# A Mamba-2 scan feeding a gated feed-forward layer: steps by pairs of sequences in the first block, scans spread over the block's end, one more row set by TensorE, the first weight piece in halves, the later pieces converted in the loop

## The chip, the cores and the metric

One core of one Trainium2 chip. The metric is the device time of one execution in microseconds (us), the median of several executions. The profile counts from the core's first to its last instruction, about 1.8 us less than the time of the same execution. All positions below are us from the start of that span. TensorE is called PE in the profile, VectorE DVE, ScalarE ACT, GpSimd POOL, the queue that issues transfers SP.

## The reference, cut to what matters

```python
# attention part: x (4, 8, 768, 32), a (4, 8, 768), B and C (4, 8, 768, 16), float32
for c in range(nc):                              # chunks along the sequence
    L = exp(cum[i] - cum[j]) * causal            # products of a between j and i
    y_intra = ((C @ B.T) * L) @ x
    y_inter = (C @ state) * exp(cum)
    state   = decay_full * state + sum(B x decay_from_j)
# bridge: (batch, head, seq, dim) -> x of shape (3072, 256)
h = x @ w_in                                     # w_in (256, 2048), stored as float64
g = h * cos(h)
return g @ w_out                                 # w_out (2048, 256), stored as float64
```

The weights arrive as float64. They are turned into float32 on the chip with integer operations, piece by piece, before TensorE can use them.

## The kernel before: the parts that the change and the argument touch

The 768 positions are six blocks of 128. A block holds the four sequences, 512 tokens. It has 16 steps: in step n a first product `h = x w_in` for 128 (block 0) columns of w_in or for two times 128 columns and two of four sequences (later blocks), then k, w, sin and the gate on ACT and DVE, and two steps later (LAG = 2) the second product with w_out. The argument follows each engine's instructions in program order; on what that rests is said in point 3 of the section on the prediction.

A weight piece is 2 of 16 column blocks; in0, in1 are the first pieces of w_in, out0, out1 those of w_out. A hole is a time in which TensorE waits. A fill is a matmul on ones whose result nobody uses; it only keeps TensorE busy. yT is ACT's copy of the scan's output, which the first product reads. `grade` puts Abs and `last` on ACT and a clip on POOL, `join` two operations on DVE and an add on POOL:

```python
def grade(which, i, later=False):
    ...
    ACT.activation(mag, high.bitcast(FP32), AF.Abs)
    G.tensor_scalar(out=mag, in0=mag, scalar1=MOST, scalar2=LEAST, op0=ALU.min, op1=ALU.max)
    ...
    def rest():
        ACT.activation(last, low, AF.Copy, scale=2.0 ** -29)
def join(which, i):
    ...
    V.tensor_scalar(out=bits, ..., op0=ALU.logical_shift_left, op1=ALU.bitwise_and)
    V.scalar_tensor_tensor(out=bits, in0=high, scalar=0xC0000000, in1=bits, ...)
    G.tensor_tensor(out=dst.bitcast(U32), in0=bits, in1=last, op=ALU.add)
order = [(w, i) for i in range(NPC) for w in ("in", "out")]     # in0 out0 in1 out1 ...
```

The end of the prologue and the loop:

```python
    join(*order[0])                 # in0
    grade(*order[2])                # in1
    intra(0, 3)
    finish(0, 2, "o", 1)
    grade(*order[1])                # out0
    finish(0, 3, "o", 2)            # all four sequences of block 0 are done here
    fill(...)
    join(*order[2])
    join(*order[1])
    ...
    for n in range(NC * NF + LAG):
        ...
        first(n)
        if n == 1:
            ...                     # sum_up of chunk 0
        if n + 3 < len(order):
            rest = grade(*order[n + 3], later=True)
        if n + 2 < len(order):
            join(*order[n + 2])     # out1 in step 1, in2 in step 2, out2 in step 3 ...
        gate(n)
        ...
        if n >= LAG:
            second(n - LAG)
        if c + 1 < NC:              # scan of the next chunk: a sequence each 3 steps, from step 2
            b, j = divmod(f - 3, 3)
            ...
```

## Time and profile before

| what | value |
|---|---|
| time, median of 3 at first (4 with the change's runs) | 397.08 (397.11) us |
| the execution that was traced | 399.58 us, span 397.8, mean granted clock 0.988 |
| TensorE busy | 388.4 us, 98% |
| first product of step 0 in the trace | 24.79 |
| first second product in the trace | 31.52 |

The prediction below shows the page, the chain of waits, the start and the clock. A busy TensorE column counts latency that overlaps with the next matmul (a product of L457 has a mean of 384 ns on the page, but eight of them take 1.73 in the chain), so lengths are taken from the chain, where pieces stand end to end.

### The profile page before, as it was taken

The page shows a single profiled execution, that of the slowest core. Times are in us where ns is not written, and L with a number is a line of the kernel's source. Part 1 is how long each engine was busy: PE and PEld are TensorE (multiplying, and loading weights), DVE is VectorE, ACT ScalarE, POOL GpSimd, SP SyncE. Part 2 cuts the span into 40 slices and gives each one's busy share as a digit, 9 for nine tenths or more (in the row PEclk, how much of TensorE's full clock was granted, in tenths as well). Part 3 has the DMA queues.
Part 4 walks back from the last instruction along what each step waited for, and adds up shares of the span by engine and source line. Part 5 has one row for each costly group of instructions (what it writes and reads, how often), then busy time and mean ns, then how long its engine had stood idle before and what let it go on. Part 6 is the DMA issues. An engine that isn't in the chain of part 4 may idle for free.

```text
span 397.8 us, 7670 instructions
## 1 busy us (share of the span) xinstructions
PE 388.4 (98%) x2926; PEld 321.5 (81%) x2926; DVE 266.4 (67%) x411; ACT 177.9 (45%) x341; POOL 248.0 (62%) x369
## 2 busy tenths in 40 slices
PE   8899999999999999999999999999999999999994
PEld 3446666669889889998889988889988888999994
DVE  7659999974877764776763677773676774444443
ACT  3746666534444344443443433444344443444431
POOL 5556657893665854966764775774665673665751
PEclk9889999999999999999999999999999999999998
DMA  9989799977000398100199000081010010010101
GB/s 100 236 219 238 202 261 175 190 124 97 20 2 0 95 198 80 28 2 0 47 231 95 18 11 0 2 231 35 2 28 0 2 26 2 2 26 2 27 3 26
DMA packets 107365, 30.69 MB, mean 77 GB/s; under 512 B 76512, under 2 KB 103232, under 8 KB 107328
## 3 DMA queue, kind: packets, MB, share of 16 engines
q1 hardware_dynamic: 106272, 29.94, 37.6%
q10 hardware_dynamic: 1056, 0.26, 0.4%
q8 instruction: 23, 0.38, 0.4%
q14 instruction: 14, 0.11, 0.1%
HBM read 26.85 MB, written 3.34 MB: 76 GB/s over the span
## 4 chain that ended last, share of the span: by engine, by line
PE 79%; DVE 10%; issue 4%; ACT 3%; SPq 2%; DMA 1%; DVEq 0%; ACTq 0%
PE hp L457 36%; PE o L548 31%; PE g L370 3%; PE y L402 3%; DVE w L463 2%; SPq L118 2%; PE y L393 2%; DVE gT L470 1%; PE o L512 1%; DVE mag L204 1%; DVE lam L338 1%; DMA bc<-in_C_dram 1%; DVE mag L206 1%; PE hp L447 1%; ACT w L468 1%
## 5 line engine op out<-in xcount | busy, mean ns | idle before, releaser
L457 PE MATMUL hp<-yT,w_in 128*128 128x256 f32 x640 | 154.6, 384 | 0.0
L457 PEld LDWEIGHTS hp<-yT,w_in 128*128 128x128 f32 x640 | 115.5, 190 | 19.8 <-issue 6.1
L496 POOL TENSOR_TENSOR gd<-gT 128x256 f32<-128x256 f32 x79 | 70.8, 896 | 96.6 <-DVE gT L470 96.6
L470 DVE TENSOR_TENSOR gT<-hp,w 128x512 f32<-128x512 f32 x96 | 66.3, 690 | 71.3 <-ACT w L468 69.2
L468 ACT ACTIVATE w<-w,quarter 128x512 f32<-128x512 f32 x96 | 69.3, 722 | 89.1 <-DVE w L463 89.1
L461 ACT ACTIVATE k<-hp 128x512 int32<-128x512 f32 x96 | 57.4, 598 | 105.5 <-PE hp L457 98.9
L463 DVE SCALAR_TENSOR_TENSOR w<-hp,k 128x512 f32<-128x512 f32 x96 | 65.6, 683 | 46.4 <-ACT k L461 45.8
L548 PE MATMUL o<-words,gd 128*128 128x128 f32 x480 | 66.7, 275 | 0.0
L548 PEld LDWEIGHTS o<-words,gd 128*128 128x128 f32 x480 | 60.0, 192 | 0.0
L338 DVE TENSOR_TENSOR_SCAN lam<-arow,unit 128x512 f32<-128x512 f32 x40 | 57.5, 1439 | 0.0
L498 POOL TENSOR_TENSOR gd<-gT,gd 128x128 f32<-128x128 f32 x79 | 49.5, 627 | 6.2
L548 PEld LDWEIGHTS o<-w_out,gT 128*128 128x128 f32 x320 | 48.2, 191 | 4.4 <-DVE ps L562 0.3
L548 PE MATMUL o<-w_out,gT 128*128 128x128 f32 x320 | 49.0, 275 | 0.1
L499 POOL TENSOR_TENSOR gd<-gT,gd 128x128 f32<-128x128 f32 x79 | 36.0, 456 | 6.2
L383 DVE TENSOR_TENSOR m<-g,lam 128x512 f32<-128x512 f32 x48 | 30.7, 680 | 3.0 <-POOL mag L186 1.9
L512 PEld LDWEIGHTS o<-w_out,gT 128*128 128x128 f32 x128 | 24.3, 190 | 9.3 <-issue 6.7
L447 PE MATMUL hp<-yT,w_in 128*128 128x512 f32 x64 | 30.9, 608 | 0.7 <-DVE gT L470 0.7
L548 PE MATMUL o<-w_out,gd 128*128 128x128 f32 x160 | 30.9, 275 | 0.0
L548 PE MATMUL o<-words,gT 128*128 128x128 f32 x160 | 30.9, 275 | 0.0
L512 PE MATMUL o<-w_out,gT 128*128 128x256 f32 x128 | 30.2, 379 | 0.0
L548 PEld LDWEIGHTS o<-words,gT 128*128 128x128 f32 x160 | 24.3, 192 | 0.0
L548 PEld LDWEIGHTS o<-w_out,gd 128*128 128x128 f32 x160 | 24.3, 192 | 0.0
(90 smaller groups left out, 345.1 us busy)
## 6 DMA issues: line engine op xcount, KB each, us to landing
arow<-a_cut SPq DMA_DIRECT2D x20, 512.0 KB
words<-in_moe_w_in_dram SPq DMA_DIRECT2D x8, 512.0 KB
words<-in_moe_w_out_dram SPq DMA_DIRECT2D x8, 512.0 KB
out_dram<-sum SPq DMA_DIRECT2D x20, 128.0 KB
xr<-in_x_dram SPq DMA_DIRECT2D x4, 512.0 KB
along<-a_all SPq DMA_DIRECT2D x20, 64.0 KB
xr<-in_x_dram SPq DMA_DIRECT2D x8, 128.0 KB
bc<-in_B_dram SPq DMA_DIRECT2D x4, 256.0 KB
```

What stands on the lines that cost most here:

```text
L338: V.tensor_tensor_scan(out=lam[c, b][:, hs].rearrange("p h i -> p (h i)"), data0=rows_.rearrange("p h i -> p (h i)"), data1=unit.rearrange ...
L447: PE.matmul(hp[n], lhsT=w_in[:, k, f * P:(f + 1) * P], rhs=yT[c][:, k], start=(k == 0), stop=(k == KT - 1))
L457: PE.matmul(to_[:, e], lhsT=w_in[:, k, fs], rhs=y[:, k, u], start=(k == 0), stop=(k == KT - 1), skip_group_check=True)
L461: ACT.activation(k, hp[n], AF.Copy, bias=0.25, scale=INV_2PI)
L463: V.scalar_tensor_tensor(out=w, in0=hp[n], scalar=INV_2PI, in1=k, op0=ALU.mult, op1=ALU.subtract)
L468: ACT.activation(cos, cos, AF.Sin, bias=quarter, scale=TWO_PI)
L470: V.tensor_tensor(out=gT[n], in0=hp.pop(n), in1=cos, op=ALU.mult)
L496: E.tensor_tensor(out=d[:, 0:2], in0=g[:, 1:2].to_broadcast([P, 2, P]), in1=g[:, 3::-3], op=ALU.subtract)
L498: E.tensor_tensor(out=d[:, 2], in0=g[:, 0], in1=d[:, 0], op=ALU.subtract)
L499: E.tensor_tensor(out=d[:, 3], in0=g[:, 2], in1=d[:, 2], op=ALU.subtract)
L512: PE.matmul(o[c][b], lhsT=g[:, b * P:(b + 1) * P], rhs=w_out[:, f], start=(f == 0 and b % 2 == 0), stop=(f == NF - 1), skip_group_check=True)
L548: PE.matmul(at[q], lhsT=a_[q], rhs=w[q], start=(j == 0 and q in starts), stop=(j == NJ - 1), skip_group_check=True)
```

## The change

Its intent: step 0 needs only sequences 0 and 1 if a step takes the tokens of one pair of sequences, as in the later blocks, so the feed-forward part can begin before sequence 3 is ready. The first weight piece in halves makes that early start possible. All rows of `a` for chunk 0 are spread by TensorE instead of one by a broadcast load. Scans of later chunks move towards the end of the block and over it. And the pieces after the first are converted in the loop, each near the step that uses it. The diff, cut to its core:

```diff
-    fill(warm[:, 0:2])
+    spread_a(0, "h")
     ...
-    grade(*order[0]) ... join(*order[0]); grade(*order[2]) ... grade(*order[1]); finish(0, 3, "o", 2)
-    fill(...); join(*order[2]); join(*order[1])
+    grade("in", 0, n=2)                  # two halves
+    ...
+    join("in", 0); finish(0, 2, "o"); intra(0, 3)
     ...
+    piece = {n: ("out", n // 2) if n % 2 else ("in", n // 2 + 1) for n in range(NF)}
+    FROM, EACH = 7, 4
+    EARLY = 4
     for n in range(NC * NF + LAG):
         first(n)                         # block 0: sequences 0, 1 in even steps, 2, 3 in odd ones
-            join(*order[n + 2])
-            gate(n)
+            for m in ((n,) if n < EARLY else ()) + ((n + 1,) if n >= EARLY - 1 else ()):
+                rests.append(grade(*piece[m], later=True))
+            if n >= EARLY and n in piece:
+                join(*piece[n])
+            gate(n)
+            for r in rests: r()
+            if n < EARLY:
+                if n == 0:
+                    first_scan()         # sequence 3's y, its copy on ACT, the sums of chunk 0
+                join(*piece[n])          # in1 in step 0, out0 in step 1, in2, out1
         ...
-            b, j = divmod(f - 3, 3)      # scans
+            c, j = divmod(n + 1 - FROM - EACH * b, NF)   # four steps each, from step 6
```

## The prediction

> **What bounds the kernel now.** I read the page first (busy shares, clock, costliest groups), then the busy times by window, then the timeline of the first 50 us, then the chain of waits. All times are us from the span's start unless marked ns.
>
> The page, engine shares and the rows of the matmuls:
> ```profile
> PE 388.4 (98%) x2926; PEld 321.5 (81%) x2926; DVE 266.4 (67%) x411; ACT 177.9 (45%) x341; POOL 248.0 (62%) x369
> ...
> L457 PE MATMUL hp<-yT,w_in 128*128 128x256 f32 x640 | 154.6, 384 | 0.0
> ...
> L447 PE MATMUL hp<-yT,w_in 128*128 128x512 f32 x64 | 30.9, 608 | 0.7 <-DVE gT L470 0.7
> ...
> L512 PE MATMUL o<-w_out,gT 128*128 128x256 f32 x128 | 30.2, 379 | 0.0
> ```
> TensorE is the bound. The means include latency that overlaps, so a matmul's cost is read from the chain of waits instead, where a stream's pieces stand end to end:
> ```profile
> 104.24 1.56 PE o L548 x14
> 105.80 0.64 PE g L370 x8
> 106.44 1.92 PE hp L457 x8
> 108.37 1.56 PE o L548 x14
> 109.93 0.38 PE y L393 x8
> 110.30 0.57 PE y L402 x16
> 110.88 0.11 PE s_ps L419 x8
> 110.99 1.93 PE hp L457 x8
> ...
> 114.48 0.11 PE tp L351
> 114.58 0.11 PE tp L352
> 114.69 1.73 PE hp L457 x8
> ```
> From block 1 on there is no hole: one piece starts where the other ends. Eight records of 256 columns cost 1.73; a sequence's scan costs TensorE 0.22 + 0.64 + 1.06 and two slower starts of 0.19, together 2.3. A block-0 step is a first product of 1.73 (four records of 512, or eight of 256: the same) and a second of 1.73, so 3.46. Four scans in a block are 9.2. These are matmuls that the change only moves. So time can come only from the start, from holes in block 0, and from the clock.
>
> The start, in the timeline (third column engine, then line):
> ```profile
> 16.93 1.08 PE L402 MATMUL y<-m,xr 128*32 128x128 f32 x16
> 18.02 1.73 PE L370 MATMUL g<-cT,bcT 32*128 32x256 f32 x8
> ...
> 24.79 3.67 PE L447 MATMUL hp<-yT,w_in 128*128 128x512 f32 x8
> ...
> 29.73 1.96 PE L447 MATMUL hp<-yT,w_in 128*128 128x512 f32 x4 [0.69 <-DVE gT L470]
> ...
> 31.52 1.89 PE L512 MATMUL o<-w_out,gT 128*128 128x256 f32 x8
> ```
> The first product of step 0 starts at 24.79, those of step 2 at 29.73, the second product of step 0 at 31.52. From step 2 to block 1's first product (88.4) are 58.7; the work in it is 14 steps of 3.46 and 9.2 of scans, 57.6. So block 0 has only about 1 us of holes after 29.73 and 0.9 before. The same stretch keeps VectorE full too, and here is the clock:
> ```profile
> 16.00:17.00 1.00, 1.00 (x13) 0.38 (x16) 0.00 (x0) 0.89 (x4) 0.86 (x3) 0.70 0.83 279
> 22.00:23.00 1.00, 1.00 (x3) 0.82 (x4) 0.69 (x1) 1.00 (x3) 0.00 (x0) 0.50 1.05 393
> 30.00:35.00 5.00, 5.00 (x17) 2.88 (x16) 4.93 (x11) 4.11 (x7) 2.75 (x3) 1.00 0.99 262
> 50.00:60.00 10.00, 10.00 (x67) 5.89 (x66) 9.53 (x17) 7.06 (x14) 5.26 (x7) 1.00 0.95 261
> ```
> Columns: length, busy PE, PEld, DVE, ACT, POOL, then granted clock, DMA share, GB/s. DVE is 9.53 of 10 in 50 to 60; the clock was 0.50 from about 16.4 to 23.
>
> **What the skill says.** (1) "TensorE: Matmul & The Clock Gate", What's actually happening: the array's clock is halved after an idle window of about 3.4 us and restored after a busy one. The trace agrees: it fell after a hole at 14.1 to 15.3 amid small row- and column-tiled matmuls, and rose at 23.1 after the fills. (2) Same page, Architectural detail: ScalarE and VectorE are strict first-in-first-out, only weight loads are pulled ahead. The trace agrees: step 1's ACT k (29.32) waits behind the weight conversion's "last" (28.77), although its matmuls ended at 28.3. So I can schedule by program order. (3) "SBUF — State Buffer", Who interferes with whom: VectorE and GpSimd exclude each other on a shared port pair; L204 takes 409 to 1485 ns here, 416 median, which fits.
>
> **The change, part by part.**
>
> *Prologue.* A separate row0 (256 KB, whose wait cost VectorE 1.00 at 6.35) goes; sequence 0 is spread by TensorE as the others. I put the first scan some 0.35 earlier (6.6 for 6.95), the four at 1.14 end at 11.15, and m of sequence 0 is done at 12.4, of sequence 1 at 13.7 (before 15.05: TensorE no longer stands at the third turn). The a_in load is moved behind, and with row0 gone sequence 3's B lands 1 to 2 earlier than 15.28. Then ACT sets the pace: turn 2's copies end near 15.0, the first piece in halves (four of about 0.37) 16.5, yT of sequence 1 at 17.3, turn 3's copies 18.2, then intra 3 (0.65), which stands ahead of step 0 in TensorE's queue. VectorE joins the halves at 16.75 to 17.95, GpSimd adds (half of 1.27 each) to 18.75: just hidden. First product of step 0: T = 19.3 with a full clock, 20.3 with half. Gain: 5.5, less 0.65 for sequence 3's y, which now follows step 0: 4.85.
>
> *Steps 0 to 6, the new latency.* Before, pieces in0, in1 and out0 were all joined before step 0 or right at it. Now in1 is joined in step 0, out0 in step 1, in2 in 2, out1 in 3, each after that step's gate. One link each from the trace: first product 1.73 and 0.22 until ACT sees it, k 0.6, w 0.7, sin 0.76, gate 0.7, join 0.42 + 0.69, add 1.27 and 0.15 of hand-overs; Abs and last 0.67 each on ACT. Relative to T:
> - Step 0: k to 2.55, Abs to 3.2, sin to 4.0, last to 4.7, and only then the copy of yT for sequence 3, to 5.0. Step 1 multiplies sequences 2 and 3, so it starts at 5.1. TensorE ended its sums at 3.05: hole 2.0.
> - in1's add ends at 7.3; step 2's product starts 7.4: hole 0.4. It ends at 9.15.
> - Step 1: product to 6.9, gate to 9.9, out0 joined to 11.0, added to 12.4. The second product of step 0 stands next in the queue: hole 3.3, start at 12.5, so 31.8 absolute against 31.52 before. The whole earlier start is used up here.
> - Step 3: product 14.2 to 16.0, two Abs ahead of its sin, gate to 19.6, out1 added 22.1; the second product of step 2 could start at 19.45: hole 2.6.
> - From step 4 the join stands ahead of the gate; out2 (step 5) still comes 0.4 late.
> - Later, VectorE has per four steps 4 x (0.68 + 0.69 + 1.37) + 5.3 of scan = 16.3 against TensorE's 4 x 3.46 + 2.3 = 16.1: balanced; I allow 1.5 for out pieces a little late.
>
> Sum of holes 10.2. Before's holes in the same stretch were 1.9.
>
> *Scans moved.* Sequences 2 and 3 of each later chunk go into the next block's first half, which needs only sequences 0 and 1. TensorE's 2.3 per sequence is then paid there: 0 net. VectorE is relieved at the end of block 0, where the holes were only the 1 us credited above. The last block's tail is the same code.
>
> *Cut rows.* a_cut leaves some 10 later, so transfers pause near 21 to 29; what follows is 9.8 MB, at 235 GB/s 42, done near 70; each piece and chunk-1 row is needed 10 or more after it lands. Hidden.
>
> Sum with a full clock: -4.85 + 10.2 - 1.9 = +3.45.
>
> *Clock.* The prologue stays thin on TensorE and has one fill instead of five, so I expect the half clock again around 16.4: T 1.0 later and the first product 1.7 longer, 2.7, taken at 0.6: +1.6. The holes of 2 and 3.3 may bring it down once more; about +2 at half a chance: +1. That makes +6; since the change keeps step order, buffers and constants tuned, I leave 0.6 for what I don't see in it: **+5.4, 402.5 us.**
>
> **Rivals.** *The earlier start carries through:* if out0 and in1 came ready sooner than I have it (ACT and VectorE back to back take some 0.1 less per instruction than their records), the holes shrink to 4 and the result is 392 to 395. For it: all engines have spare time in 20 to 30 (VectorE 5.47 of 10). Against: it is a chain of dependences, not of busy time. *VectorE is the bound of block 0*, and moving two scans out (10.6 of VectorE's time) frees as much: 390 to 393. For it: VectorE stands in most of the chain from 30 to 84. Against: TensorE had its next piece back to back in 46 to 75, so it can't go faster. *The clock falls twice or more:* each fall halves the rate for some 3.4 to 7; 406 to 409. For it: fewer fills, longer holes. Against: 28.2 to 29.7 was thin too and kept 1.00. *Late weights by DMA:* would add several us, but nothing in before waits for a piece longer than 0.2.
>
> **Range and chances.** From 396 (half of my holes don't appear, clock mostly full) to 408 (all appear and two falls). Faster by 2% needs 389.1, more than the start and all holes of block 0 together would plausibly give: 0.05. Slower by 2% is over 405.0, my sum plus one fall of the clock: 0.29. Within: 0.66.
>
> **What would show it.** Step 0's first product near 19 to 21; a TensorE hole ended by POOL's add into w_out before the first second product (near 32) and another before that of step 2; step 1 released by the ACT copy of yT; block 1's first product near 93, with two scans still to come; blocks 1 to 4 at 61.9 each as before; the clock at 0.5 around 17 to 23. I am wrong if the first second product starts before 29, if the holes are under 4 together, or if a later block's length changes by over 0.5.

## The result, and the profile after

407.38 us (406.68 to 408.06, 4 runs) against 397.11. The ratio is 1.0259, 95% interval 1.0237 to 1.0282: slower. Ratios here are the mean time of one kernel's fast runs over the mean of the other's fast runs of the same rounds, so they are not quite the ratio of the medians quoted beside them.

The page of the changed kernel, the engine shares and the two groups of products, to be compared with the lines of the prediction:

```profile
PE 387.3 (95%) x2986; PEld 332.4 (82%) x2986; DVE 263.2 (65%) x410; ACT 178.2 (44%) x343; POOL 249.3 (61%) x373
...
L462 PE MATMUL hp<-yT,w_in 128*128 128x256 f32 x768 | 187.6, 388 | 2.0 <-ACT yT L411 2.0
...
L519 PE MATMUL o<-w_out,gT 128*128 128x256 f32 x128 | 32.3, 397 | 9.3 <-POOL w_out L217 9.3
```

No engine has much more to do; only the weight loads (PEld) grow, by 10.9 us, and e5 below finds no cost in that. TensorE has 11.3 us of waits that were not there: 2.0 for a copy of yT, 9.3 for POOL's add into w_out. (Gone are 2.0 of before's: 0.7 for gT, 1.3 for transfers in the prologue.) The chain of waits of the changed kernel shows how the first two come about (start, length, what; "issue" is a hand-over):

```profile
18.52 2.09 PE hp L462 x8
20.61 0.02 issue
20.63 0.61 ACT k L466
21.24 0.02 issue
21.26 0.70 DVE w L468
21.96 0.02 issue
21.99 0.72 ACT w L473
22.71 0.55 ACT last L191
23.26 0.26 ACT yT L411
...
26.54 0.61 ACT k L466
...
28.68 0.57 issue
29.26 0.43 DVE mag L207
29.69 0.02 issue
29.71 0.70 DVE mag L209
...
30.55 1.28 POOL w_out L217
```

Step 0 starts at 18.45, over 6 us before the traced kernel's 24.79. But step 1 needs the yT copy, which stands behind Sin and `last` in ACT's order. And the first second product needs out0, whose join stands behind step 1's gate in DVE's order. In the timeline of TensorE, the second products that wait (length of the wait in brackets):

```profile
31.87 3.38 PE L519 MATMUL o<-w_out,gT 128*128 128x256 f32 x8 [2.89 <-POOL w_out L217]
42.67 2.00 PE L519 MATMUL o<-w_out,gT 128*128 128x256 f32 x8 [2.23 <-POOL w_out L217]
50.50 2.00 PE L519 MATMUL o<-w_out,gT 128*128 128x256 f32 x8 [0.66 <-POOL w_out L217]
77.47 2.00 PE L519 MATMUL o<-w_out,gT 128*128 128x256 f32 x8 [2.47 <-POOL w_out L217]
94.20 2.00 PE L519 MATMUL o<-w_out,gT 128*128 128x256 f32 x8 [0.33 <-POOL w_out L217]
```

The first of them starts at 31.87; before it started at 31.52. The early start is gone by the time the second products begin. The one at 31.87 also takes 3.38 instead of 2.00. The windows show why (busy time of PE, PEld, DVE, ACT, POOL, then granted clock, DMA share, GB/s):

```profile
20.00:24.00 4.00, 2.05 (x53) 1.53 (x52) 1.92 (x4) 2.70 (x5) 0.61 (x1) 1.00 0.32 117
24.00:28.00 4.00, 4.00 (x13) 3.16 (x12) 1.38 (x3) 1.26 (x3) 1.99 (x4) 0.57 0.10 27
28.00:32.00 4.00, 1.11 (x6) 0.66 (x4) 2.58 (x6) 2.92 (x6) 1.83 (x3) 0.91 0.92 197
32.00:36.00 4.00, 4.00 (x13) 3.31 (x14) 1.98 (x5) 0.58 (x2) 1.66 (x2) 0.66 0.83 216
```

In this trace the clock is down after each of these two stretches in which TensorE had little to do (2.05 of 4, then 1.11 of 4). The hole of 2.23 ahead of 42.67 was not followed by a fall.

The wait of 2.47 at 77 has its own history, in the timeline of POOL:

```profile
70.71 1.27 POOL L217 TENSOR_TENSOR w_in<-mag,last 128x512 uint32<-128x512 uint32 x1 [0.63 <-DVE mag L209]
71.94 1.40 POOL L494 TENSOR_TENSOR words<-w_out 128x512 f32<-128x512 f32 x1
73.31 1.52 POOL L194 TENSOR_SCALAR mag<-mag 128x512 f32<-128x512 f32 x1
76.15 1.26 POOL L217 TENSOR_TENSOR w_out<-mag,last 128x512 uint32<-128x512 uint32 x1 [1.32 <-DVE mag L209]
```

and of DVE:

```profile
72.19 2.23 DVE L342 TENSOR_TENSOR_SCAN lam<-arow,unit 128x512 f32<-128x512 f32 x1
```

A difference of w_out (L494) and a clip that takes 1.52 instead of 0.61 run against a scan that takes 2.23 instead of 1.2: POOL and DVE hold each other up there, as the Trainium skill, "SBUF — State Buffer", Who interferes with whom, describes for a DVE instruction with two SBUF inputs and a POOL instruction that reads SBUF. The trace agrees: the scan ends 1.08 after the difference (74.42 and 73.34), about what it takes elsewhere, and the clip ends 0.41 after the scan. The join follows late, and with it TensorE; e8 tests how much of that is due to the differences.

### The profile page after: what moved, and what is told of

Its sections match the earlier page's. It is cut to its first block, busy times and chain, and to the rows that moved or that the text cites. A ratio compares the mean times of both kernels' runs of the same rounds, so it can differ in the third digit from the quotient of the medians.

```text
span 406.1 us, 7789 instructions
## 1 busy us (share of the span) xinstructions
PE 387.3 (95%) x2986; PEld 332.4 (82%) x2986; DVE 263.2 (65%) x410; ACT 178.2 (44%) x343; POOL 249.3 (61%) x373
## 4 chain that ended last, share of the span: by engine, by line
PE 87%; DVE 4%; ACT 3%; POOL 2%; issue 2%; DVEq 0%; POOLq 0%; ACTq 0%
PE hp L462 39%; PE o L554 30%; PE o L519 4%; PE g L374 4%; PE y L406 3%; PE y L397 2%; POOL w_out L217 1%; ACT w L473 1%; DVE w L468 1%; DVE mag L209 1%; PE a_ps L298 1%; ACT k L466 1%; PE warm L101 1%; PE tp L355 1%; DVE lam L342 1%
## 5 line engine op out<-in xcount | busy, mean ns | idle before, releaser
L462 PE MATMUL hp<-yT,w_in 128*128 128x256 f32 x768 | 187.6, 388 | 2.0 <-ACT yT L411 2.0
L462 PEld LDWEIGHTS hp<-yT,w_in 128*128 128x128 f32 x768 | 140.2, 192 | 27.2 <-issue 7.4
L501 POOL TENSOR_TENSOR gd<-gT 128x256 f32<-128x256 f32 x79 | 79.9, 1011 | 91.6 <-DVE gT L475 86.4
L342 DVE TENSOR_TENSOR_SCAN lam<-arow,unit 128x512 f32<-128x512 f32 x40 | 56.0, 1399 | 0.0
L503 POOL TENSOR_TENSOR gd<-gT,gd 128x128 f32<-128x128 f32 x79 | 44.8, 567 | 6.2
L519 PE MATMUL o<-w_out,gT 128*128 128x256 f32 x128 | 32.3, 397 | 9.3 <-POOL w_out L217 9.3
L504 POOL TENSOR_TENSOR gd<-gT,gd 128x128 f32<-128x128 f32 x79 | 36.0, 455 | 6.2
L194 POOL TENSOR_SCALAR mag<-mag 128x512 f32<-128x512 f32 (+1 forms) x17 | 12.8, 752 | 17.2 <-ACT mag L193 17.2
```

What stands on the lines that cost most here:

```text
L342: V.tensor_tensor_scan(out=lam[c, b][:, hs].rearrange("p h i -> p (h i)"), data0=rows_.rearrange("p h i -> p (h i)"), data1=unit.rearrange ...
L462: PE.matmul(to_[:, e], lhsT=w_in[:, k, fs], rhs=y[:, k, u], start=(k == 0), stop=(k == KT - 1), skip_group_check=True)
L501: E.tensor_tensor(out=d[:, 0:2], in0=g[:, 1:2].to_broadcast([P, 2, P]), in1=g[:, 3::-3], op=ALU.subtract)
L503: E.tensor_tensor(out=d[:, 2], in0=g[:, 0], in1=d[:, 0], op=ALU.subtract)
L504: E.tensor_tensor(out=d[:, 3], in0=g[:, 2], in1=d[:, 2], op=ALU.subtract)
L519: PE.matmul(o[c, u][:, t], lhsT=g[:, 2 * e + t], rhs=w_out[:, 2 * j + e], start=(j == e == t == 0), stop=(j == NJ - 1 and e == 1), skip_gr ...
```

## The experiments

Twelve kernels ran, all correct. One thing has to be said first. **The executions of one kernel fall in two groups by their mean granted clock.** In the rounds of all experiments the kernel before took 396.4 to 397.7 us in 28 runs with a clock of 0.996 or more, and 399.2 to 400.4 in 11 runs with 0.988 to 0.990; nothing lies between (one run of 997 us is left out, it was marked slow). The split is made by looking at the clock after the run, so a comparison within one group shows what a kernel takes in that state, not whether its change brings the state about. The changed kernel took 406.7 and 406.8 at 0.997, 407.9 and 408.1 at 0.988. All of these count as fast runs. So I compare times of equal clock where less than 3 us matter. The trace of the kernel before is of the slower group.

The start scatters too, with the same code. The changed kernel, e1, e2, e3, e8, e11 and e12 share everything ahead of step 0 except, in e3, e11 and e12, the conversion of in1 and two more fetches; their traces have step 0 between 18.45 and 20.32. Between the changed kernel (18.45) and e1 (19.95) the whole 1.5 is there by 7.4 us: the same first four products that spread `a` take 1.02 in the one chain and 1.91 in the other. In e11 (and e6) the clock is at half from about 15 to 18.5. So a start from one trace is good to about 1 us, and the rows below are read with that in mind.

Marks on the way, in the traces (us). "Block 1" is where its first second product starts. Kernels with spread scans have one scan, 2.3, still to do there:

| kernel | time of that run, clock | step 0 | first second product | block 1 |
|---|---|---|---|---|
| before | 399.58, 0.988 | 24.79 | 31.52 | 97.28 |
| changed | 407.92, 0.988 | 18.45 | 31.87 | 103.31 |
| e1 fills | 407.27, 0.997 | 19.95 | 32.73 | 102.67 |
| e2 scan first | 405.28, 0.997 | 19.08 | 30.63 | 100.67 |
| e3 ahead | 395.55, 0.997 | 19.06 | 26.68 | 90.95 |
| e4 spread only | 399.08, 0.988 | 24.58 | 31.31 | 94.48 |
| e5 alternate only | 397.06, 0.998 | 22.12 | 28.80 | 94.57 |
| e6 ahead, whole piece | 396.75, 0.995 | 20.38 | 27.83 | 92.16 |
| e7 late joins on before | 411.02, 0.983 | 24.65 | 35.15 | 108.74 |
| e8 differences later | 410.16, 0.988 | 19.37 | 31.86 | 105.52 |
| e9 row 0 only | 396.11, 0.996 | 21.20 | 27.93 | 93.69 |
| e10 ahead, turn 3 early | 395.94, 0.997 | 19.34 | 27.08 | 91.34 |
| e11 ahead, late copy | 399.22, 0.991 | 20.32 | 30.51 | 94.62 |
| e12 ahead, unspread | 396.11, 0.997 | 19.45 | 27.06 | 93.81 |

The theory after the result: the pieces of w_in and w_out are joined too late in the first steps, the holes cost more than the early start brings, and the clock lengthens a little what is left. Rivals: the clock is the main loss; the spread scans cost as such; the alternation costs as such.

### e1: fills in the holes

```diff
+    warm = bank([P, 4, P], "warm", "o"); fill(warm, 2)     # step 0, after the sums
+    if n == 2: fill(warm, 4)                               # ahead of the first second product
+    if n == 4: fill(pair("warm")..., 2)                    # ahead of the third
```

> The changed kernel with fill matmuls (operands all ones, results unused) in three of its TensorE holes: two in step 0, four ahead of the first second product, two ahead of the third; nothing else moves. Theory (late weight pieces make the holes, the falling clock only lengthens the matmuls between them by 3.3 in all): the granted clock stays 1.00 from 5 us on, the holes that wait for GpSimd's add into w_out remain, and the time falls by 2 to 3.5 us, to about 404.5. Rival (the clock is the main cause of the loss of 10): the time falls by 6 or more, to 401 or less. Rival (the clock loss is hidden behind the latency chain): within 0.7 us of 407.4.

Measured: 407.41 us (406.82 to 407.60), clock 0.993 to 0.997. The clock stayed up as wanted in the trace, and the time did not move. By the times the expectation of 2 to 3.5 us less failed, and the third reading, a hidden loss, held. The wait ahead of the third second product is now

```profile
42.03 1.99 PE L519 MATMUL o<-w_out,gT 128*128 128x256 f32 x8 [0.52 <-POOL w_out L217]
```

with 1.9 of fills ahead of it: filled, but still as late. Against the changed kernel's own runs at 0.997 it is even 0.7 longer. But its step 0 started at 19.95, 1.5 late for a reason that the edit does not touch (see above). From step 0 to block 1 it took 82.72, the changed kernel 84.86: 2.1 less, within what I had expected. So whether the loss by the clock is hidden, or the fills brought 2 and a slower start took most of it away, these runs do not settle. The clock is not the main cause either way: with it up, e1 still needs 82.72 where e5 (below) needs 72.45. As an estimate, the falls cost the changed kernel between the 1.2 us that part its two groups and these 2.1.

### e2: sequence 3's copy first in step 0

```diff
             first(n)
+            if n == 0: first_scan()
             ...
-                if n == 0: first_scan()
```

> The changed kernel with one move: sequence 3's y, its copy on ScalarE and the sums stand straight behind step 0's first product in program order, so the copy that step 1 waits for no longer queues behind the Abs, Sin and last of the weight conversion. Theory (program order on ScalarE sets step 1's start): step 1 starts about 1.9 us earlier (21.7 for 23.57), out0 is joined some 2.5 earlier, and the time falls by 2 to 3, to about 404.7; the hole before the third second product stays at 2 to 2.5. Rival (weight pieces alone set the pace, the copy is beside the path): step 2 still waits for the second piece of w_in and the time falls by less than 0.7.

Measured: 407.33 us, but in two groups, 405.28 and 405.37 at a clock of 0.997, 409.28 and 409.63 at 0.986. At equal clock it gains 1.4 us against the changed kernel: less than I expected, more than the rival did. Step 1 started 3.2 after step 0 instead of 5.1, as expected, and then the next wait stood there:

```profile
22.30 1.99 PE L462 MATMUL hp<-yT,w_in 128*128 128x256 f32 x8
26.68 1.99 PE L462 MATMUL hp<-yT,w_in 128*128 128x256 f32 x8 [2.39 <-POOL w_in L217]
30.63 1.99 PE L519 MATMUL o<-w_out,gT 128*128 128x256 f32 x8 [1.95 <-POOL w_out L217]
```

The hole of 2.0 turned into one of 2.39 for in1. Taking one wait away showed the one behind it. (In the lower group e2 is 1.5 over the changed kernel's; only the upper group was traced.)

### e3: every piece one place earlier

```diff
     intra(0, 3)
+    grade("in", 1)
+    join("in", 1)
     ...
-            for m in ((n,) if n < EARLY else ()) + ((n + 1,) if n >= EARLY - 1 else ()):
+            for m in ((n + 1,) if n < EARLY else ()) + ((n + 2,) if n >= EARLY - 1 else ()):
-            if n >= EARLY and n in piece: join(*piece[n])
+            if n >= EARLY and n + 1 in piece: join(*piece[n + 1])
             ...
-                join(*piece[n])
+                join(*piece[n + 1])
```

with the move of e2 and two pieces fetched ahead of the loop.

> The changed kernel with every weight piece converted one place earlier in the step order: the second piece of w_in before step 0 (ScalarE and VectorE stand idle there), out0 in step 0 and so on, and the move of the run before this one; two pieces are fetched before the loop instead of in it. Alternation, spread scans, halves and row 0 by TensorE stay. Theory (the loss is the late joins, the earlier start is worth what was predicted): the first second product starts near 26 (31.9 in the changed kernel, 31.5 in the one before), holes waiting for w_out shrink under 3 in all, the clock stays up, and the time is 391 to 395, below the kernel before. Rival (spread scans or the alternation cost as such): it stays over 398. Rival (weights by DMA are the next wait): a hole on ScalarE waiting for a words transfer of over 1 us appears, and the time is 396 to 400.

Measured: 395.41 us (395.02 to 395.77), ratio to before 0.9936 (0.9887 to 0.9985). That is 12 us less than the changed kernel with all of its other parts kept. Three edits made it: the earlier pieces, e2's move, and the two fetches that the first needs. e11 takes the move out again and is still 10.2 us below the changed kernel, so the earlier pieces are the main part. The fetches were not tried alone, but in the changed kernel no wait of ACT, DVE or POOL from 15 to 105 is for the transfer of a piece. It lies 0.4 over the 391 to 395 that I gave. The waits of TensorE up to 105 us, kernel e3:

```profile
PE g L374 <- ACT bcT L362: 1.8, 3, 0.9
PE o L519 <- POOL w_out L217: 0.6, 2, 0.4
PE y L397 <- DVE m L387: 0.2, 1, 0.2
```

and of the changed kernel in the same stretch:

```profile
PE o L519 <- POOL w_out L217: 9.3, 6, 2.9
PE hp L462 <- ACT yT L411: 2.0, 1, 2.0
PE g L374 <- ACT bcT L362: 1.3, 2, 0.9
```

9.3 became 0.6, and 2.0 became 0. Against the kernel before at equal clock (396.5 to 397.2 in these rounds) the gain is 1.5 us. The traces fit: step 0 starts 3.06 before e5's 22.12, the first second product 2.12 before e5's, and at block 1 1.3 are left (90.95 and the 2.3 of a scan against 94.57).

### e4: spread scans alone, on the kernel before

```diff
-            b, j = divmod(f - 3, 3)
+            c, j = divmod(n + 1 - FROM - EACH * b, NF)      # FROM, EACH = 7, 4
```

> The kernel before with one part of the change alone: the scans of the later chunks in groups of four steps from step 6 on, so that two of four sequences' scans run in the next block. Theory (TensorE's work is only moved, 0 net): 396.5 to 398 us. Rival (VectorE bounds block 0 and is relieved): 394 to 396. Rival (the spread costs, through GpSimd and VectorE getting in each other's way in steps 9 to 12): 398.5 or more.

Measured: 398.49 us (398.06 to 399.08), ratio 1.001 (0.9952 to 1.0069), a little over the 396.5 to 398 of the theory. At 0.996 to 0.998 it is 1.4 over the runs of before of that clock, at 0.988 (one run) it is under them. So no part of the 10 us is shown to be here, and the sign is open.

### e5: alternation alone, on the kernel before

```diff
-        if c == 0:
-            for k in range(KT):
-                PE.matmul(hp[n], lhsT=w_in[:, k, f * P:(f + 1) * P], rhs=yT[c][:, k], ...)
-        else: ...
+        u, j = turn_of(n)
+        for e in range(2):
+            for k in range(KT):
+                PE.matmul(to_[:, e], lhsT=w_in[:, k, fs], rhs=y[:, k, u], ...)
```

and the second product of block 0 accordingly.

> The kernel before with one part of the change alone: block 0's steps alternate between the two pairs of sequences (products of 256 columns instead of 512, the outputs in two accumulators by pair); the start, the joins and the scans stay. Theory (it only regroups the same TensorE work; by itself it neither starts earlier nor costs anything): 396.5 to 398 us at the same mean clock. Rival (the smaller products and twice as many weight loads of the first product cost some 0.1 each step): 398.5 to 399.5.

Measured in five rounds: 396.90 us, ratio 0.9994 (0.9961 to 1.0027). The alternation costs nothing that these runs show. Since its start is the code of the kernel before, its trace also shows the start of before with the clock up (timeline of TensorE):

```profile
22.12 3.62 PE L458 MATMUL hp<-yT,w_in 128*128 128x256 f32 x16
...
28.80 1.89 PE L515 MATMUL o<-w_out,gT 128*128 128x256 f32 x8
```

22.12, where the trace of before has 24.79.

### e6: e3 with the first piece whole

```diff
-    grade("in", 0, n=2)
+    grade("in", 0)
```

> The kernel with every piece converted one place earlier (third run of the first set, 395.4), with the first piece converted whole instead of in halves. Theory (that kernel has almost no holes, so a later start of step 0 shows in full; the halves bring 0.4 to 0.9): step 0 starts 0.6 to 0.9 later and the time is 395.8 to 396.3. Rival (the halves cost as much in extra instructions as they hide): 395.4 or less.

Measured: 396.73 us (395.97 to 396.97), 1.3 over e3 (in other rounds), more than the 0.4 to 0.9 expected. In the trace step 0 started at 20.38 instead of 19.06, but that is not shown to be due to the whole piece: the clock was at half from about 15 to 18.5, step 0 did not wait for w_in (the add ended at 20.06), and e11, with the piece in halves and the same fall of the clock, started at 20.32. So the halves seem to be worth about 1 us in time; by what path, this trace does not show.

### e7: late joins alone, on the kernel before

```diff
-    grade(*order[2]); grade(*order[1]); join(*order[2]); join(*order[1])     # in1, out0 ahead of the loop
     ...
-                rest = grade(*order[n + 3], later=True)
-                join(*order[n + 2])
+            (grade and join in the steps and places of the change: piece, EARLY = 4;
+             the last four differences of w_out one step later, since they need the last piece)
```

> The kernel before with one thing of the change alone: the weight pieces after the first are converted and joined in the order and at the steps of the changed kernel (second piece of w_in in step 0, first of w_out in step 1, after the gate up to step 3), two differences of w_out two steps later because they need the last piece; start, fills, block-0 steps and scans stay. Theory (late joins are the loss, wherever they stand): TensorE waits for GpSimd's add into w_in or w_out before step 2 and before the first and third second products, 5 to 9 in all, and the time is 402 to 407 us. Rival (late joins hurt only together with the alternation, where step 1 waits for a copy): under 399.

Measured: 410.61 us (410.02 to 411.14), ratio 1.0325 (1.0284 to 1.0366), at a clock of 0.983 to 0.986. It is the strongest single piece of evidence: this part alone, put on the kernel before, costs 13.5 us, more than the whole change. Not all of that is the joins: its trace has the half clock in the prologue that only the slower group of before has (0.51 from 16 to 20, before's trace 0.55). The two traced executions are the fair pair, 411.02 against 399.58, and 11.4 are left. My 402 to 407 was too low; the rival, under 399, is out. (The expectation speaks of two differences moved by two steps; the edit moves four by one.) Against the trace of before, which has the same start (24.65, 24.79), the first second product is 3.6 later and block 1 11.5 later. The waits of TensorE:

```profile
PE o L512 <- POOL w_out L210: 5.9, 6, 2.0
PE hp L447 <- POOL w_in L210: 3.1, 1, 3.1
```

and the clock is down again in 32 to 40, where the products behind these waits run:

```profile
32.00:36.00 4.00, 3.44 (x6) 1.41 (x7) 2.61 (x6) 1.63 (x4) 1.89 (x3) 0.65 0.99 186
36.00:40.00 4.00, 4.00 (x9) 2.78 (x9) 3.22 (x6) 1.27 (x2) 1.75 (x2) 0.50 1.03 309
```

The first in time, at 31.97, is the one for in1, as in e2.

### e8: the differences of w_out later

```diff
-    differ_at = {NF - 7: (0, fore), NF - 6: (1, fore), NF - 5: (2, fore), NF - 4: (3, fore), ...
+    differ_at = {NF - 2: [(0, fore), (1, fore)], NF - 1: [(2, fore), (3, fore)], NF: [(0, hind)], ...
```

> The changed kernel with GpSimd's differences of w_out (four of 128x512 in steps 9 to 12, four in 15 to 18) moved to steps 14, 15 and 16 to 19, behind the last joins but one. Theory (the hole of 2.6 at 75 us comes from GpSimd: a difference and a clip that wait for VectorE's port pair stand ahead of the add of that step): the hole shrinks to under 1.2 and the time falls by 1 to 2 us at the same mean clock. Rival (VectorE's scans and joins in one step are the cause, 2.2 for a scan that takes 1.2 elsewhere): the hole stays over 2 and the time within 0.7.

Measured: 411.42 us, from 406.87 at a clock of 0.996 to 412.7 at 0.980. At the high clock (one run) that is the changed kernel's time: no gain. The hole did shrink, and another came where the differences went:

```profile
78.40 1.99 PE L519 MATMUL o<-w_out,gT 128*128 128x256 f32 x8 [1.43 <-POOL w_out L217]
...
96.41 1.99 PE L519 MATMUL o<-w_out,gT 128*128 128x256 f32 x8 [1.60 <-POOL w_out L217]
```

1.43 for 2.47, and 1.60 for 0.33: the sum is 3.03 against 2.80, and all waits for w_out together are 9.6 against 9.3. The scan that took 2.23 takes 1.19 here (at 74.17), and the hole of 1.43 that stays has another part in it, which no run takes apart. POOL's differences were a part of the cause; moving them moved it. In e3 they stand where the change has them and nearly nothing waits, because the pieces have a step of slack.

### e9: row 0 by TensorE alone, on the kernel before

```diff
-    nc.scalar.dma_start(out=row0[...], in_=a[0, ...].to_broadcast([W, H, W]))     # twice
+    G.tensor_scalar(out=a0z, in0=a0, **clip); G.memset(a0z[:, 0:P:W], 0.0)
+    spread_a(0, "h")
```

> The kernel before with one part of the change alone: no separate row of sequence 0, all rows of a spread by TensorE, the copy with zeroed first columns made by GpSimd. Theory (it frees 256 KB of the first transfers, but step 0 waits for TensorE's queue of turns, scans and fills, set by sequence 3's B and C): step 0 starts 0 to 1 us earlier than 22.1 (where the run of the alternation alone, with the same start and the clock up, had it) and the time is 396.0 to 397.2 at a mean clock of 0.997 or more. Rival (the prologue is bound by the first scans): 1.5 us or more earlier and 395.5 or less. Rival (one more spread by TensorE costs): 397.5 or more at that clock.

Measured: 396.44 us (396.11 to 396.70), all four runs at 0.996 or 0.997. Step 0 started at 21.20, 0.9 before e5's. At equal clock (before: 396.7 to 397.4 in these rounds) it gains some 0.7. In the same rounds 6 of 11 runs of before were in the slow-clock group and none of these four; four runs are few to say that the part keeps the clock up.

### e10: e3 with sequence 3's transposes earlier

```diff
     turn(0, 2, "h")
+    turn(0, 3, "h")
     grade("in", 0, n=2)
     ...
-    turn(0, 3, "h")
```

> The kernel with every piece converted one place earlier (395.4), with sequence 3's transposes and their copies placed straight behind sequence 2's, ahead of the first piece's conversion on ScalarE, since step 0 waits for them. Theory (ScalarE's order in the prologue sets the start of step 0, 19.06 there, and TensorE has no holes left behind it): step 0 starts 0.4 to 0.9 us earlier, 18.2 to 18.7, and the time is 394.4 to 395.1, faster than the kernel before at the same clock by 1.5 to 2.5. Rival (the first piece is then late by as much): no earlier start, 395.2 or more.

Measured in five rounds: 395.40 us (394.93 to 395.94), the same as e3. Step 0 did not start earlier:

```profile
19.34 2.28 PE L462 MATMUL hp<-yT,w_in 128*128 128x256 f32 x8 [0.40 <-POOL w_in L217]
```

It waits for the first piece now. The rival was right; my reading is that the copies for sequence 3 and the conversion of the first piece share ACT, and that what one gains the other loses. The ratio to before is 0.9924 (0.9893 to 0.9955), but 6 of the 11 runs of before in these rounds were in the slow-clock group; at equal clock the gain is some 1.8 us.

### e11: e3 with the late copy

```diff
             first(n)
-            if n == 0: first_scan()
             ...
+                if n == 0: first_scan()
                 join(*piece[n + 1])
```

> The kernel with every piece converted one place earlier (395.4), with sequence 3's y, copy and sums put back where the change has them, behind step 0's gate and weight conversion. Theory (with the pieces ready, that copy's place in ScalarE's queue is a hole of its own): step 1 starts 1.7 to 2.1 us later behind a hole that the copy ends, and the time is 396.5 to 397.5, the gain over the kernel before gone. Rival (the later slack takes it in): under 395.9.

Measured: 397.19 us (396.97 to 399.22), 1.8 over e3, with the hole where it was expected:

```profile
25.30 5.37 PE L462 MATMUL hp<-yT,w_in 128*128 128x256 f32 x16 [1.96 <-ACT yT L411]
```

At a clock of 0.996 in both it is 397.2 against e3's 395.3: with the pieces ready, that copy's place costs its full 2 us. In e2, with the pieces late, the same move brought 1.4.

### e12: e3 with the scans closer together

```diff
-    FROM, EACH = 7, 4
+    FROM, EACH = 6, 3
```

> The kernel with every piece converted one place earlier (395.4), with the later chunks' scans in groups of three steps from step 5, so that all but the last two parts of the fourth sequence fall inside the block as in the kernel before. Theory (spreading only moves TensorE's work and its effect on VectorE is small: 13.6 of VectorE against 12.7 of TensorE per three steps, some of it absorbed): 395.2 to 396.5 us at a mean clock of 0.996 or more. Rival (without the spread VectorE bounds the block): 397 or more, TensorE holes that wait for VectorE or for w_out of over 2 us between 50 and 90. Rival (the spread is itself a loss): 394.8 or less.

Measured in five rounds: 396.10 us (395.13 to 396.99), 0.7 over e3, as the theory had it. The two ran in different rounds and their runs overlap, so that the spread helps here is likely but not shown; e4 had it the other way by 1.4 or nothing. Its share of the 10 us is small in either case.

## Why the prediction was right or wrong, point by point

The prediction said slower, 402.5 us in a range of 396 to 408; it was 407.4. It gave 0.29 to a loss of over 2% and 0.66 to a time within 2%; the loss was 10.3, twice its 5.4. The mechanism was right; two terms of the sum were mis-sized, the gain too large (point 2) and the later holes too small (point 4).

1. **"First product of step 0: T = 19.3 with a full clock."** The trace has 18.45, and kernels with the same start have 19.37 (e8) and 19.95 (e1). Right, and so is its 20.3 for the half clock: e11 has 20.32 with it.
2. **"Gain: 5.5."** Wrong in size: this is the first step of the sum that failed. I took the start of before, 24.79, from the trace of an execution with 399.58 us, and then added the difference to the median of 397.08. With the clock up the same start is at 22.12 (e5). The gain was 3.7 against the changed kernel's trace and 2.2 to 2.8 against the starts of e1 and e8, not 5.5. The page showed the half clock from 16.4 to 23, and I read it as the normal state of the kernel before. In 28 of 39 runs it seems not to be: 6.7 us at half clock are 0.0084 of the span, which is the step from 0.997 to 0.988, and 22.12 for 24.79 is the step of 2.6 us between the groups. (Only one execution of that start with the clock up was traced.)
3. **The holes of steps 0 to 6.** Predicted 2.0, 0.4, 3.3, 2.6, 0.4; measured 1.95, none, 2.89, 2.23, 0.66. The one of 0.4 for in1 disappeared because steps 1 and 2 ran at half clock in the trace; in e8, where they did not, it is 0.39. The first second product was predicted at 31.8 and came at 31.87. That this fits to 0.1 is luck in part: the start was 0.85 earlier than predicted, and the half clock made the way from there 0.9 longer (13.42 for 12.5). In e8, with the clock up on that way, it took 12.49. This was scheduling by program order, one link after the other, and it held. It rests on ACT and DVE being strictly first in, first out, the Trainium skill's "TensorE: Matmul & The Clock Gate", Architectural detail; e2 (against the changed kernel) and e11 (against e3), which change only the order, agree with it: step 1 moves from 5.1 to 3.2 after step 0, and back to 5.0.
4. **"Later ... I allow 1.5 for out pieces a little late."** Wrong in size: 0.69, 2.47 and 0.33, together 3.5. This is the second term that failed. I had weighed DVE's busy time against TensorE's and found them equal, and left out that a POOL difference, a clip and a scan in one step delay each other by more than their means. For the 2.47 the trace and e8 support that in part; the two small ones were not looked into.
5. **The clock.** I expected it down at 16.4 and perhaps once more, 2.6 in the mean. In the trace it stayed up until 24, then fell twice. The products of steps 1 and 2 take 5.41 where e3 has 3.97, and the first second product 3.38 where it has 1.99. The net effect on the time is estimated at 1.2 (the two groups) to 2.1 (e1's way from step 0 to block 1); so the 2.6 was somewhat high, and the places were wrong. The prediction also says that the trace agrees with an idle window of about 3.4 us. That is too strong: the fall at 16.4 followed a hole of 1.2, and e5 has much the same hole and no fall.
6. **"TensorE's 2.3 per sequence is then paid there: 0 net."** From block 1's first second product to the end the changed kernel takes 302.8 us, e5 300.6. The difference, 2.2, is the one scan still to do. Blocks 1 to 3 take 61.9 each in both kernels and block 4 61.5 and 61.6, as predicted, so the whole loss lies ahead of block 1. The spread as such moved the time by 1.4 at most (e4), in the other direction in e12.
7. **"Cut rows ... Hidden."** Right: no wait of TensorE in the changed kernel after step 0 is for a transfer.
8. **The rivals.** That the start carries through, and that DVE bounds block 0, both fell. e3 shows under which condition the start does carry through: the pieces have to come forward with it.

The sum once more, changed kernel against e5 (407.92 and 397.06, difference 10.9): the start 3.7 earlier; from there to the first second product 13.4 instead of 6.7; to block 1 71.4 instead of 65.8; to the end 2.2 more. -3.7 + 6.7 + 5.7 + 2.2 = 10.9. And the prediction's own sum with its two terms put right (a gain of 2.8 for 5.5, later pieces 3.5 for 1.5, the rest as it stands) is 10.1; measured were 10.3. Some of that is luck, since the first four holes were 7.7 together and not 8.7, and the clock fell elsewhere. What stays open is the sign of the spread scans' small effect, what the falls of the clock cost by themselves, and what decides in which clock group a run falls.

## What to carry to other kernels

An early start is worth only as much as the slowest thing that the next few steps need: bring the inputs of those steps forward too, or the stream waits for them and ends up where it was. Read the lag between a step and the first use of its result along each engine's program order, link by link; busy shares do not show it: here ACT, DVE and POOL were busy for 44 to 65% of the span, and TensorE waited for their chain all the same. And before taking a duration from a trace, compare the traced execution's own time and clock with the median: here they belonged to different groups, 2.5 us apart.

## What the Trainium skill lacked or had wrong

- "TensorE: Matmul & The Clock Gate", What's actually happening, says that a busy window of about 3.4 us restores the clock, not what counts as busy, nor how much of a window must be idle for a fall. In the kernel before, TensorE's busy column is full while the clock stays at half for some 6.7 us; there the matmuls are the small ones of the scan, on 32 rows or into 32 columns, and fills on the whole array. In e5, whose code is the same up to step 0, it did not fall. And in the changed kernel it fell after a gap of only 1.95. Two windows of before's trace, then of e5's (the clock is the third figure from the end):

```profile
16.00:20.00 4.00, 3.99 (x34) 2.27 (x34) 2.78 (x5) 2.49 (x7) 1.29 (x4) 0.55 0.96 342
20.00:24.00 4.00, 4.00 (x38) 2.33 (x37) 2.20 (x5) 1.50 (x3) 2.52 (x4) 0.60 1.06 349
...
16.00:20.00 4.00, 3.54 (x51) 1.89 (x51) 3.20 (x6) 2.30 (x7) 1.74 (x4) 1.00 0.98 319
20.00:24.00 4.00, 4.00 (x34) 3.16 (x32) 3.08 (x5) 2.08 (x5) 3.21 (x4) 1.00 1.04 359
```

- The same page calls the warm-up run-variable and its penalty under 1% of a typical span. Our runs agree in size (2.5 us of 397; 4.1 of 405 in e2, just over 1%), but it lacks the consequence for measuring: one program on one core has two groups of times, 396.4 to 397.7 and 399.2 to 400.4 us for the kernel before, 405.3 and 409.5 for e2. A mean over both hides or invents 1%.
- "SBUF — State Buffer", Who interferes with whom, has the rule that DVE with two SBUF inputs and a reading POOL exclude each other, but no figure for a scan. Here the same 128x512 scan takes 1.24 us in the median and 2.23 beside POOL, and the POOL clip 0.61 at the least and 1.52 beside the scan.
